# Four of the seven layer-1 products of the last four batches as seven inner products each

## The chip, the cores and the metric

The kernel runs on one core of a Trainium2 chip. The metric is the device time of one execution in microseconds (us); the times are medians of a few runs. All arithmetic is in 32-bit floats.

## The reference

An attention block with pooled queries is followed by a block in which each batch routes its 128 best tokens through a two-layer network.

```python
# attention: B, H, S, D = 8, 8, 1152, 64
q_pool = q.reshape(B, H, S // 2, 2, D).mean(axis=3)
attn = softmax(q_pool @ k^T / sqrt(D))
x = (attn @ v) as (B, 576, 512)
# mixture of depths: w1 is 512 x 1024, w2 is 1024 x 512, capacity 128
scores = np.einsum('bsd,d->bs', x, w_gate)
out = x.copy()
for b in range(B):
    top_idx = np.argpartition(-scores[b], capacity)[:capacity]
    xe = x[b, top_idx]
    h = np.maximum(xe @ w1, 0.0)
    ye = h @ w2
    g = 1.0 / (1.0 + np.exp(-scores[b, top_idx]))
    out[b, top_idx] = x[b, top_idx] + g[:, None] * ye
```

## The kernel before

The attention runs over 32 pairs of heads in two halves each (`run`); it takes some 572 us, and TensorE is busy all through. While it runs, the gate scores of each batch are summed, its tokens ranked, gathered (L1179) and turned into `xeT`, features on the partitions. The network of all eight batches is computed at the end, in `ending`, and this is the part that the change touches.

`ending` takes the batches in two groups of four, and in each group two pairs of batches form the two block rows of a matrix. A product of 2 x 2 blocks is made with seven block products instead of eight (Winograd's form of Strassen's method), with four sums of the inputs (S1 to S4), four sums of the weights (T1 to T4, made during the attention and kept in `tw` and, for layer 2, in `last_sums`), and seven additions of the results.

- Layer 1 of a group (`first_layer`): block rows are two pairs of batches, block columns of the input the two halves of the 512 features, block columns of the weights two halves of the 1024 hidden units. One block product (`first_product`, matmuls at L1271) has an input of 2 chunks x 128 features by 256 tokens and weights of 256 x 512. It is 8 matmuls of 128 x 128 weights and 256 columns, and a 32-bit matmul shows as two passes in the trace: 16 passes. Each product fills one PSUM tile of two banks. VectorE adds the results (`add`, L1298), ScalarE copies the first (L1311) and applies Relu to each finished quarter c11, c12, c22, c21 (L1309).
- Layer 2 (`second_of`, matmuls at L1285): for a pair of batches, seven products of 8 passes, 128 tokens by 256 outputs. ScalarE copies some (L1362, L1364), VectorE adds, multiplies by the gate and adds to the tokens (`scaled`, L1293). The last pair is written out at the end of `ending`.
- `input_sums` makes S1 to S4 of layer 1 on GpSimd (POOL, L1257); `four_sums` makes those of layer 2 on VectorE (L1351).
- `scattered` writes a pair's tokens to the output by two indirect DMAs of POOL (`written`, L1240).

PSUM holds four product tiles (`banks`, a pool of four buffers of two banks), taken in turn: a fifth product waits until the first one's tile is read. The order on every engine is the order in which the program issues (`manual_schedule`); the order is written out by hand, and `pieces` interleaves it: it steps through the generator of a layer, and at the steps numbered in `behind` it also issues a piece of the ranking of the last batch (`waiting`), whose last step is the transpose that completes the tokens of batch 7 (L1215). `counted` (L1511) and `outside` (L1526, a matmul of one column) test the softmax sums of all batches for a range; a rerun in another form follows if they leave it.

Most SBUF is used, so the rooms of the ending are tiles of the attention's pools taken again: `rooms[0]` and `rooms[1]` (two tiles of exponents) hold the quarters of the hidden layer, intermediate sums and the input sums of layer 2; `acc` holds the input sums of layer 1 and the intermediate results of layer 2.

Of the kernel before, what the change touches and what calls it, by code (L numbers as in the profile page):

```python
# [540 lines left out]
class _Plain:  # L541
# [707 lines left out]
    def input_sums(self, a, s):  # L1249

        a11, a12, a21, a22 = a
        s1, s2, s3, s4 = s
        add, subtract = ALU.add, ALU.subtract
        for to, x, y, op in (
            (s1, a21, a22, add), (s2, s1, a11, subtract), (s3, a11, a21, subtract), (s4, a12, s2, subtract)
        ):
            self.nc.gpsimd.tensor_tensor(out=to, in0=x, in1=y, op=op)  # L1257

# [38 lines left out]
    def add(self, to, x, y):  # L1297
        self.nc.vector.tensor_tensor(out=to, in0=x, in1=y, op=ALU.add)  # L1298
# [54 lines left out]
    def second_of(self, tokens, a, s, y):  # L1353

        copy, add = self.nc.scalar.copy, self.add
        half, w = self.Dm // 2, tokens[0]["w"]
        y1, y2, y7, y3, y4 = (y[0:w, i * half : (i + 1) * half] for i in range(5))
        to = [token["xe"][0:w, i * half : (i + 1) * half] for token in tokens for i in range(2)]
        one, two = tokens
        products = self.second_layer(a, s, (1, 2, 7, 3, 4, 5, 6))  # L1360
        for part in (y1, y2, y7):
            copy(part, next(products))  # L1362
            yield
        copy(y3, next(products))  # L1364
        add(y2, y2, y1)
        self.scaled(to[0], y2, one, to[0])
        yield
        add(y4, y1, next(products))
        add(y3, y3, y4)
        add(y4, y4, y7)  # L1370
        yield
        ps = next(products)
        add(y4, y4, ps)
        add(y7, y3, ps)
        yield
        add(y3, y3, next(products))
        for of, at, token in ((y3, to[1], one), (y4, to[2], two), (y7, to[3], two)):
            self.scaled(at, of, token, at)
        yield

    def ending(self, halves, old):
# [7 lines left out]
        def pieces(unit, n=None, of=1):  # L1389
            nonlocal done  # L1390
            for i, _ in enumerate(unit):
                for _ in range(of):
                    if done in behind:
                        next(waiting)
                    done += 1
                if i + 1 == n:
                    break
# [10 lines left out]
        def first(i):  # L1408
            x, y = (self.tokens[4 * i + 2 * j]["turned"] for j in range(2))
            a = [t[:, :, k * self.ND // 2 : (k + 1) * self.ND // 2, 0:w] for t in (x, y) for k in range(2)]  # L1410
            c = [self.hidden_of(rooms[i][:, k * n : (k + 1) * n], w) for k in range(4)]
            m = [self.hidden_of(room[:, 4 * n : 5 * n], w) for room in rooms]
            return a, c, self.first_layer(a, inputs, c, m)

        def second(i, j, c):
            a = [c[2 * j + k][:, :, t, :] for t in range(2) for k in range(2)]
# [15 lines left out]
        a, c, layer = first(0)  # L1432
# [9 lines left out]
        self.scored(halves[-1])  # L1442
        _, new, _ = self.routing.pop()
# [13 lines left out]
        pieces(self.second_of(*y, acc[1]))  # L1457
        a, c, layer = first(1)
        self.input_sums(a, inputs)
        self.scattered(y[0])  # L1460

        pieces(layer, 2)
        low = self.counted()
        pieces(layer, 2)
        outside = self.outside(low)
        pieces(layer, 1)
        x, y = second(1, 0, c), second(1, 1, c)
        self.four_sums(*x[1:])
        pieces(layer)
        layer = self.second_of(*x, acc[1])  # L1470
        pieces(layer, 3)
        self.four_sums(*y[1:])
# [221 lines left out]
```

## Time and profile before

| | us |
|---|---|
| median of the runs | 673.01 |
| lowest and highest run | 672.97, 673.38 |
| the profiled execution: time | 673.65 |
| the profiled execution: span | 671.9 |
| first layer-1 product of the second group starts, in the span | 617.40 |
| last product of TensorE ends, in the span | 666.2 |
| last scatter issued by POOL, in the span | 667.06 |

The span runs from the first to the last instruction of one execution; its time, 1.7 us longer, holds what lies around the span. PE is TensorE's matmuls and PEld its weight loads, which overlap them; DVE is VectorE, ACT ScalarE, POOL GpSimd, SP the engine that issues most DMAs. Times in the trace are us from the span's start. "[2.56 <-DVE acc L1298]" after an instruction says that its engine stood idle for 2.56 us before it and what ended the wait.

### The profile page before, as it was taken

To read this page: it belongs to the slowest core of one execution; us is meant where nothing else is said; L and a number is where in the kernel's file an instruction comes from. 1 tells how busy PE (TensorE), PEld (TensorE's weight loads), DVE (VectorE), ACT (ScalarE), POOL (GpSimd) and SP (SyncE) were. 2 spreads that over 40 slices of the span, in tenths; PEclk is the share of its full clock that TensorE was granted. 3 is DMA by queue.
4 is the path that set the end of the run, shared out by engine and by line. 5 is a ranking of instruction groups with operands and counts; after the bars stand their busy time and mean duration, and the time that the engine had idled before them with its cause. 6 is when DMAs were issued, how large, how long until landed. Compare 5 with 4: busy or idle time off the path is not lost.

```text
span 671.9 us, 22869 instructions
## 1 busy us (share of the span) xinstructions
PE 665.1 (99%) x9715; PEld 438.4 (65%) x9715; DVE 565.2 (84%) x811; ACT 441.2 (66%) x959; POOL 499.8 (74%) x465
## 2 busy tenths in 40 slices
PE   9999999999999999999999999999999999999996
PEld 6656666666666666666666666656666666888885
DVE  3878999998999987998899888988898899596463
ACT  5677778777777777778777777777777874221120
POOL 5788888889888988899888978898889877302302
PEclk9999999999999999999999999999999999999999
DMA  8989989868886788859866879588958845303001
GB/s 164 169 178 194 216 173 189 150 113 179 159 154 117 122 163 153 166 105 177 170 117 130 170 137 149 127 160 146 156 112 163 153 139 151 73 16 105 33 2 66
DMA packets 391048, 92.68 MB, mean 138 GB/s; under 512 B 371608, under 2 KB 376088, under 8 KB 390936
## 3 DMA queue, kind: packets, MB, share of 16 engines
q1 hardware_dynamic: 389496, 86.73, 67.1%
q0 software_dynamic: 1280, 4.20, 1.7%
q8 instruction: 78, 1.28, 0.8%
q14 instruction: 34, 0.28, 0.2%
q10 hardware_dynamic: 160, 0.20, 0.1%
HBM read 75.30 MB, written 15.79 MB: 136 GB/s over the span
## 4 chain that ended last, share of the span: by engine, by line
PE 92%; issue 5%; DMA 2%; POOL 1%; DVE 0%; POOLq 0%
PE ps L878 42%; PE ps L896 42%; PE ps L1285 4%; PE ps L1271 4%; DMA out_dram<-xe,index 1%; PE ps L623 1%; DMA out_dram<-v_sb,index 0%; POOL acc L1257 0%; POOL out_dram L1240 0%; PE ps L844 0%; DVE xe L1293 0%; POOL kT L1257 0%; DVE v_sb L1215 0%; PE ps L830 0%; DVE acc L1298 0%
## 5 line engine op out<-in xcount | busy, mean ns | idle before, releaser
L885 ACT ACTIVATE p<-ps 128x576 f32<-128x576 f32 x576 | 320.5, 699 | 2.2 <-PE ps L878 1.9
L917 POOL TENSOR_TENSOR acc<-p 128x576 f32<-128x576 f32 x192 | 283.0, 1501 | 38.3 <-ACT p L885 36.9
L878 PE MATMUL ps<-qT,kT 64*64 64x288 f32 x4608 | 292.0, 403 | 0.0
L896 PE MATMUL ps<-p,v_sb 64*64 64x288 f32 x4608 | 290.9, 403 | 0.0
L878 PEld LDWEIGHTS ps<-qT,kT 64*64 64x64 f32 x4608 | 174.1, 133 | 105.5 <-ACT p L885 13.4
L896 PEld LDWEIGHTS ps<-p,v_sb 64*64 64x64 f32 x4608 | 173.0, 133 | 106.6 <-ACT p L885 14.7
L922 DVE TRANSPOSE_TENSOR_REDUCE fold<-p 128x54 f32<-128x1728 f32 x64 | 126.3, 1974 | 44.3 <-ACT p L885 44.2
L904 ACT COPY two<-ps 128x576 f32<-128x576 f32 x64 | 40.8, 638 | 133.5 <-PE ps L896 131.6
L922 DVE TRANSPOSE_TENSOR_REDUCE fold<-acc 128x54 f32<-128x1728 f32 x64 | 124.5, 1945 | 3.7 <-POOL acc L917 3.5
L906 POOL TENSOR_TENSOR av<-two 128x288 f32<-128x288 f32 x64 | 51.3, 801 | 39.9 <-ACT two L904 39.0
L766 DVE STREAM_TRANSPOSE kT<-kb 128x1152 f32<-128x1152 f32 x31 | 73.9, 2385 | 0.0
L985 POOL TENSOR_TENSOR prod<-avb,w_gate 128x288 f32<-128x288 f32 x64 | 51.5, 805 | 0.0
L1116 DVE TENSOR_SCALAR_CACHE_REDUCE pick<-line 128x127 f32<-128x127 f32 (+4 forms) x80 | 45.2, 564 | 3.4 <-DMA line<-gate_lines 1.2
L763 POOL TENSOR_TENSOR qp<-qb 128x576 f32<-128x576 f32 (+1 forms) x32 | 43.9, 1373 | 5.5 <-DMA qb<-in_q_dram 3.9
L962 ACT ACTIVATE sums<-total,tiny 32x18 f32<-32x18 f32 x124 | 38.2, 308 | 1.9
L1240 POOL DMA_INDIRECT out_dram<-xe,index x7 | 6.9, 992 | 38.7 <-DVE xe L1293 28.2
L1021 POOL TENSOR_TENSOR x<-avb,rec 128x576 f32<-128x576 f32 x30 | 34.8, 1161 | 0.0
L1309 ACT ACTIVATE p<-p 128x1024 f32<-128x1024 f32 x8 | 8.5, 1058 | 39.0 <-DVE p L1298 33.5
L975 DVE STREAM_TRANSPOSE avb<-av 128x288 f32<-128x288 f32 x64 | 28.3, 442 | 3.8 <-POOL av L906 3.8
L1043 DVE TENSOR_REDUCE red<-prod 128x9 f32<-128x288 f32 x64 | 27.8, 435 | 2.7 <-POOL prod L985 2.7
L947 ACT COPY groups<-sum 32x36 f32<-32x36 f32 x124 | 27.2, 219 | 1.6
L1298 DVE TENSOR_TENSOR p<-p,ps 128x1024 f32<-128x1024 f32 x14 | 16.9, 1216 | 11.9 <-PE ps L1271 11.8
(103 smaller groups left out, 420.7 us busy)
## 6 DMA issues: line engine op xcount, KB each, us to landing
kb<-in_k_dram SPq DMA_DIRECT2D x124, 144.0 KB, 4.7
qb<-in_q_dram SPq DMA_DIRECT2D x124, 144.0 KB, 4.5
v_sb<-in_v_dram SPq DMA_DIRECT2D x31, 576.0 KB, 5.1
out_dram<-x SPq DMA_DIRECT2D x128, 72.0 KB, 5.0
lines<-row_rank SPq DMA_DIRECT2D x8, 640.0 KB, 4.2
w<-in_moe_w_dram SPq DMA_DIRECT2D x8, 512.0 KB, 4.7
line<-gate_lines SPq DMA_DIRECT2D x8, 351.5 KB
tw<-tw SPq DMA_DIRECT2D x4, 512.0 KB, 5.7
```

The costliest lines, as they stand in the source:

```text
L763: nc.gpsimd.tensor_tensor(out=qp[:, of, :], in0=pair["q"][:, of, 0, :], in1=pair["q"][:, of, 1, :], op=ALU.add)
L766: nc.vector.transpose(kT.rearrange("p (c i g) -> p c g i", c=self.NC, i=BLK), pair["k"].rearrange("p (g c) d -> p c g d", c=self.NC),)
L878: nc.tensor.matmul(sc[keys, j, 0:n], lhsT=pair["kT"][rows, c * P + keys.start : c * P + keys.stop], rhs=pair["qT"][rows, qs], start=True, ...
L885: nc.scalar.activation(p[:, c // G, c % G, :, :], sc[:, :, 0:n], AF.Exp, scale=self.scale)
L896: nc.tensor.matmul(av[j * self.D : (j + 1) * self.D, e, 0:n], lhsT=half["pair"]["v"][keys, j, c, :], rhs=half["p"][keys, c // G, c % G, j, :],
L904: nc.scalar.copy(two[:, :, :], av[:, :, 0:n])
L906: nc.gpsimd.tensor_tensor(out=half["av"][:, :], in0=two[:, 0, :], in1=two[:, 1, :], op=ALU.add)
L917: nc.gpsimd.tensor_tensor(out=acc[:, u, :], in0=units[:, 0, u, :], in1=units[:, 1, u, :], op=ALU.add)
L922: nc.vector.tensor_reduce(fold[:, a, :], of.rearrange("p u (m d) -> p (u m) d", d=BLK), AX.X, ALU.add, apply_transpose=True,)
L962: self.nc.scalar.activation(tot[rows, :], pair["total"][:, j * self.QB : (j + 1) * self.QB], AF.Identity, bias=self.tiny[0:BLK, 0:1],)
L985: self.nc.gpsimd.tensor_tensor(out=pair["prod"][:, ns, :], in0=pair["avb"][:, ns, :], in1=self.w_gate[:, hp : hp + 1, :].broadcast_to([P, ...
L1116: nc.vector.tensor_scalar(out=cmp[0:rows, 0 : part.stop - part.start], in0=near[0:rows, part], scalar1=sc[0:rows, t : t + 1], scalar2=None ...
```

## The change

The first group stays as it was in layer 1. In layer 1 of the second group `split` takes the place of `first_layer`. Four of its seven products (called one: a11 b11; two: a12 b21; six: S4 b22; seven: a22 T4) are themselves made as 2 x 2 block products with seven inner products each. An inner product (`inner_product`) has 128 features by 128 tokens and 256 hidden units: two matmuls of 128 columns, four passes. `inner_layer` issues the seven, in four banks of two PSUM tiles x and y, and adds them up on VectorE. The three others (S2 T2, S1 T1, S3 T3) stay whole. The inner weight sums (`inner_weights`, 16 adds on POOL into free tiles of the attention) are issued one at a time by `pieces`, from the first group's layer 1 on; the inner input sums (`inner_inputs`, four adds on POOL each) are issued as the layer goes. Larger sums of two products are added on POOL (`rest`), with Relu on ScalarE behind it. The order of products and sums in `second_of` is changed, the scatters of the first group's second pair and `counted` and `outside` are issued later, and the input sums of layer 2 for the next pair are split. Blank lines are left out.

```diff
--- before.py
+++ after.py
@@ -1246,15 +1246,77 @@
             oob_is_err=False,
         )
-    def input_sums(self, a, s):
+    def input_sums(self, a, s, which=slice(0, 4)):
         a11, a12, a21, a22 = a
         s1, s2, s3, s4 = s
         add, subtract = ALU.add, ALU.subtract
-        for to, x, y, op in (
-            (s1, a21, a22, add), (s2, s1, a11, subtract), (s3, a11, a21, subtract), (s4, a12, s2, subtract)
-        ):
+        steps = (s1, a21, a22, add), (s2, s1, a11, subtract), (s3, a11, a21, subtract), (s4, a12, s2, subtract)
+        for to, x, y, op in steps[which]:
             self.nc.gpsimd.tensor_tensor(out=to, in0=x, in1=y, op=op)
+    def quarter_rooms(self):
+        load, work = self.load, self.work
+        yield load.tile([P, self.QB, BLK], F32, name="qp", bufs=1)
+        for _ in range(2):
+            yield load.tile([P, self.Sp], F32, name="qT")
+        yield work.tile([P, self.QB, BLK], F32, name="prod", bufs=1)
+        for name in ("avb", "avb", "x", "x"):
+            yield work.tile([P, self.QB, BLK], F32, name=name)
+    def inner_weights(self, operands):
+        rooms = self.quarter_rooms()
+        n = self.F // 4
+        for operand in operands:
+            t = operand["t"] = []
+            b11, b12, b21, b22 = (operand["b"][:, k, j * n : (j + 1) * n] for k in range(2) for j in range(2))
+            for i in range(4):
+                if i % 2 == 0:
+                    room = next(rooms)
+                    room = self.row(room) if len(room.shape) > 2 else room
+                to = room[:, i % 2 * n : (i % 2 + 1) * n]
+                x, y = ((b12, b11), (b22, t[0] if t else None), (b22, b12), (b21, t[1] if i == 3 else None))[i]
+                self.nc.gpsimd.tensor_tensor(out=to, in0=x, in1=y, op=ALU.subtract)
+                t.append(to)
+                yield
+    def inner_inputs(self, operand):
+        room, w = operand["room"], operand["a"].shape[3]
+        a = [operand["a"][:, i, j, :] for i in range(2) for j in range(2)]
+        operand["s"] = [room[:, i * P : i * P + w] for i in range(4)]
+        self.input_sums(a, operand["s"])
+    def inner_product(self, tile, k, i, of, by):
+        to = tile[:, k, 2 * i * P : 2 * (i + 1) * P].rearrange("p (f n) -> p f n", n=P)[:, :, 0 : of.shape[1]]
+        for f in range(2):
+            self.nc.tensor.matmul(to[:, f, :], lhsT=by[:, f * P : (f + 1) * P], rhs=of, start=True, stop=True)
+        return to
+    def inner_layer(self, m, to, temps):
+        n = self.F // 4
+        product, add = self.inner_product, self.add
+        a11, a12, _, a22 = (m["a"][:, k, j, :] for k in range(2) for j in range(2))
+        b11, _, b21, b22 = (m["b"][:, k, j * n : (j + 1) * n] for k in range(2) for j in range(2))
+        (s1, s2, s3, s4), (t1, t2, t3, t4) = m["s"], m["t"]
+        c11, c12, c21, c22 = (to[:, 2 * i : 2 * i + 2, :] for i in range(4))
+        x, y = self.banks(), self.banks()
+        u, v = temps
+        self.nc.scalar.copy(u, product(x, 0, 0, a11, b11))
+        ps = product(y, 0, 0, s2, t2)
+        add(c11, u, product(x, 0, 1, a12, b21))
+        add(u, u, ps)
+        add(v, u, product(y, 1, 0, s1, t1))
+        ps = product(x, 1, 0, s3, t3)
+        add(c22, v, ps)
+        add(u, u, ps)
+        add(c12, v, product(y, 0, 1, s4, b22))
+        add(c21, u, product(x, 1, 1, a22, t4))
     def lines_of(self, room):
         return room.rearrange("p (c n) -> p c n", n=P)
@@ -1354,27 +1416,28 @@
         copy, add = self.nc.scalar.copy, self.add
         half, w = self.Dm // 2, tokens[0]["w"]
-        y1, y2, y7, y3, y4 = (y[0:w, i * half : (i + 1) * half] for i in range(5))
+        y1, y2, y5, y3, y4 = (y[0:w, i * half : (i + 1) * half] for i in range(5))
         to = [token["xe"][0:w, i * half : (i + 1) * half] for token in tokens for i in range(2)]
         one, two = tokens
-        products = self.second_layer(a, s, (1, 2, 7, 3, 4, 5, 6))
-        for part in (y1, y2, y7):
-            copy(part, next(products))
-            yield
-        copy(y3, next(products))
-        add(y2, y2, y1)
+        products = self.second_layer(a, s, (1, 5, 2, 7, 3, 4, 6))
+        copy(y1, next(products))
+        yield
+        copy(y5, next(products))
+        yield
+        add(y2, y1, next(products))
         self.scaled(to[0], y2, one, to[0])
         yield
+        add(y2, y5, next(products))
+        yield
+        copy(y3, next(products))
+        yield
         add(y4, y1, next(products))
+        add(y2, y2, y4)
         add(y3, y3, y4)
-        add(y4, y4, y7)
-        yield
-        ps = next(products)
-        add(y4, y4, ps)
-        add(y7, y3, ps)
+        add(y5, y5, y3)
         yield
         add(y3, y3, next(products))
-        for of, at, token in ((y3, to[1], one), (y4, to[2], two), (y7, to[3], two)):
+        for of, at, token in ((y3, to[1], one), (y2, to[2], two), (y5, to[3], two)):
             self.scaled(at, of, token, at)
         yield
@@ -1392,6 +1455,7 @@
                 for _ in range(of):
                     if done in behind:
                         next(waiting)
+                    next(weights, None)
                     done += 1
                 if i + 1 == n:
                     break
@@ -1405,15 +1469,76 @@
         def sums_room():
             return self.row(self.work.tile([P, G, 2 * self.HALF], F32, name="acc"))
-        def first(i):
-            x, y = (self.tokens[4 * i + 2 * j]["turned"] for j in range(2))
-            a = [t[:, :, k * self.ND // 2 : (k + 1) * self.ND // 2, 0:w] for t in (x, y) for k in range(2)]
-            c = [self.hidden_of(rooms[i][:, k * n : (k + 1) * n], w) for k in range(4)]
+        def halves_of(turned):
+            k = self.ND // 2
+            return turned[:, :, 0:k, 0:w], turned[:, :, k:, 0:w]
+        def first():
+            a = [half_of for token in self.tokens[0 : self.B // 2 : 2] for half_of in halves_of(token["turned"])]
+            c = [self.hidden_of(rooms[0][:, k * n : (k + 1) * n], w) for k in range(4)]
             m = [self.hidden_of(room[:, 4 * n : 5 * n], w) for room in rooms]
             return a, c, self.first_layer(a, inputs, c, m)
+        def lines(room):
+            return self.lines_of(room)[:, :, 0:w]
+        def across(room):
+            return room.rearrange("p (t f) n -> p f t n", t=2)
+        def rest(to, x, y, done=None):
+            nc.gpsimd.tensor_tensor(out=to, in0=x, in1=y, op=ALU.add)
+            if done is not None:
+                nc.scalar.activation(done, done, AF.Relu)
+        def hidden(to, x, y):
+            self.add(across(to), across(x), y)
+            nc.scalar.activation(to, to, AF.Relu)
+        def split(a):
+            u, v = (lines(room[:, 4 * n : 5 * n]) for room in rooms)
+            c11, c12, c21, c22 = c = [lines(rooms[1][:, k * n : (k + 1) * n]) for k in range(4)]
+            temps = [
+                [lines(rooms[0][:, k : k + half]) for k in (2 * n + 2 * i * half, 2 * n + (2 * i + 1) * half)]
+                for i in range(2)
+            ]
+            one, two, six, seven = operands
+            s1, s2, s3, s4 = inputs
+            t1, t2, t3, _ = (self.summed(1, i) for i in range(4))
+            x, product, add = second(1, 0, c), self.first_product, self.add
+            def layer():
+                self.inner_layer(one, u, temps[0])
+                yield
+                self.inner_layer(two, c11, temps[1])
+                yield
+                add(across(v), across(u), product(s2, t2))
+                rest(c11, c11, u, c11)
+                yield
+                add(across(c12), across(v), product(s1, t1))
+                self.input_sums(a, inputs, slice(3, 4))
+                self.inner_inputs(six)
+                self.input_sums(a, inputs, slice(2, 3))
+                self.inner_inputs(seven)
+                yield
+                self.inner_layer(six, u, temps[0])
+                yield
+                ps = product(s3, t3)
+                hidden(c22, c12, ps)
+                add(across(v), across(v), ps)
+                rest(c12, c12, u, c12)
+                yield
+                self.inner_layer(seven, c21, temps[1])
+                self.four_sums(*x[1:], slice(2, 3))
+                rest(c21, c21, v, c21)
+                yield
+            return c, x, layer()
         def second(i, j, c):
-            a = [c[2 * j + k][:, :, t, :] for t in range(2) for k in range(2)]
+            if i == 0:
+                a = [c[2 * j + k][:, :, t, :] for t in range(2) for k in range(2)]
+            else:
+                a = [c[2 * j + k][:, 4 * t : 4 * t + 4, :] for t in range(2) for k in range(2)]
             s = self.lines_in(rooms[1 - i][:, 2 * j * n : 2 * (j + 1) * n], self.NFC // 2, w, 4)
             return self.tokens[4 * i + 2 * j : 4 * i + 2 * j + 2], a, s
@@ -1429,7 +1554,7 @@
         self.drained(halves[-1])
         self.multiplied(halves[-2])
         rooms.append(exponents_room())
-        a, c, layer = first(0)
+        a, c, layer = first()
         self.input_sums(a, inputs)
         self.multiplied(halves[-1])
         self.scored(halves[-3])
@@ -1440,6 +1565,15 @@
         self.normalized(last)
         self.gated(halves[-1])
         self.scored(halves[-1])
+        operands = [
+            {"b": b, "room": room}
+            for b, room in zip(
+                (self.quarter(1, 0, 0), self.quarter(1, 1, 0), self.quarter(1, 1, 1), self.summed(1, 3)),
+                (*(rooms[0][:, k * n // 2 : (k + 1) * n // 2] for k in range(2)), rooms[0][:, n : n + n // 2],
+                 rooms[0][:, n + n // 2 : 2 * n]),
+            )
+        ]
+        weights = self.inner_weights(operands)
         _, new, _ = self.routing.pop()
         waiting = chain((None for _ in old), (None for _ in new), count())
         for of in (halves[-3]["pair"], last):
@@ -1454,21 +1588,26 @@
         self.four_sums(*y[1:])
         pieces(layer)
         self.scattered(x[0])
-        pieces(self.second_of(*y, acc[1]))
-        a, c, layer = first(1)
-        self.input_sums(a, inputs)
+        layer = self.second_of(*y, acc[1])
+        pieces(layer, 3)
+        operands[0]["a"], operands[1]["a"] = halves_of(self.tokens[self.B // 2]["turned"])
+        for operand in operands[:2]:
+            self.inner_inputs(operand)
+        pieces(layer)
+        a = [half_of for token in self.tokens[self.B // 2 :: 2] for half_of in halves_of(token["turned"])]
+        operands[2]["a"], operands[3]["a"] = inputs[3], a[3]
+        self.input_sums(a, inputs, slice(0, 2))
+        c, x, layer = split(a)
+        pieces(layer)
+        self.four_sums(*x[1:], slice(0, 2))
+        self.four_sums(*x[1:], slice(3, 4))
         self.scattered(y[0])
-
-        pieces(layer, 2)
-        low = self.counted()
-        pieces(layer, 2)
-        outside = self.outside(low)
-        pieces(layer, 1)
-        x, y = second(1, 0, c), second(1, 1, c)
-        self.four_sums(*x[1:])
-        pieces(layer)
+        y = second(1, 1, c)
         layer = self.second_of(*x, acc[1])
         pieces(layer, 3)
+        low = self.counted()
+        pieces(layer, 1)
+        outside = self.outside(low)
         self.four_sums(*y[1:])
         pieces(layer)
         self.scattered(x[0])
```

## The prediction

> **What bounds the kernel now.** I read the page's first part, then the busy time of the stretch that the change touches, then the order of instructions in it, engine by engine. The page's first part, and the two stretches from the start of the second group's layer 1 to TensorE's last product (columns: stretch, its length, busy time and count of each engine, granted clock, DMA):
>
> ```profile
> PE 665.1 (99%) x9715; PEld 438.4 (65%) x9715; DVE 565.2 (84%) x811; ACT 441.2 (66%) x959; POOL 499.8 (74%) x465
> ...
> 617.40:641.90 24.50, 24.50 (x116) 21.29 (x115) 13.74 (x22) 3.71 (x4) 7.72 (x7) 1.00 0.09 33
> 641.90:666.30 24.40, 24.32 (x113) 21.08 (x111) 13.22 (x27) 3.65 (x8) 2.93 (x3) 1.00 0.09 35
> ```
>
> TensorE has no idle time there: what is taken off its queue is won, and what makes it wait is lost in full, since only the last scatter (some 6 us) follows. The timeline of TensorE gives the products (start, length, engine, line, tiles, passes):
>
> ```profile
> 617.40 7.07 PE L1271 MATMUL ps<-xeT,w 128*128 128x256 f32 x32
> 624.30 7.07 PE L1271 MATMUL ps<-acc,tw 128*128 128x256 f32 x32
> 631.30 0.19 PE L1526 MATMUL ps<-low,ones 128*1 128x2 f32 x2
> 631.42 3.72 PE L1271 MATMUL ps<-kT,w 128*128 128x256 f32 x16
> ...
> 598.30 1.99 PE L1285 MATMUL ps<-kb,p 128*128 128x256 f32 x8
> 600.13 1.89 PE L1285 MATMUL ps<-qb,p 128*128 128x256 f32 x8
> ```
>
> Two products of layer 1 start 6.90 apart, so one takes 3.45 (16 passes of 0.216). A group of eight that starts after a wait lasts 1.99 instead of 1.89: a restart costs 0.1. The other engines in the same time, first VectorE and POOL around 618:
>
> ```profile
> 617.16 1.00 POOL L1240 DMA_INDIRECT out_dram<-xe,index  x1 [2.56 <-DVE acc L1298]
> ...
> 619.25 1.13 DVE L1215 STREAM_TRANSPOSE v_sb<-pick 128x512 f32<-128x512 f32 x1
> 620.53 1.27 POOL L1257 TENSOR_TENSOR acc<-v_sb 128x512 f32<-128x512 f32 x1 [2.38 <-DVE v_sb L1215]
> 621.88 1.27 POOL L1257 TENSOR_TENSOR acc<-acc,xeT 128x512 f32<-128x512 f32 x1
> ```
>
> POOL is held by the first group's scatters until 618.16, and batch 7's tokens are turned by 620.38; today S2 is ready at 623.15 and TensorE wants it at 624.3. Prices, from the groups and (last line) two passes of 128 columns at full clock early in the run:
>
> ```profile
> L1309 ACT ACTIVATE p<-p 128x1024 f32<-128x1024 f32 x8 | 8.5, 1058 | 39.0 <-DVE p L1298 33.5 <-DVE rank_parts L1107 5.5
> L1362 ACT COPY acc<-ps 128x256 f32<-128x256 f32 x9 | 3.1, 373 | 11.4 <-PE ps L1285 9.7 <-DVE xe L1293 1.7
> L1298 DVE TENSOR_TENSOR acc<-acc,ps 128x256 f32<-128x256 f32 x13 | 5.2, 418 | 9.2 <-PE ps L1285 9.1
> L1298 DVE TENSOR_TENSOR p<-p,ps 128x1024 f32<-128x1024 f32 x14 | 16.9, 1216 | 11.9 <-PE ps L1271 11.8
> L985 POOL TENSOR_TENSOR prod<-avb,w_gate 128x288 f32<-128x288 f32 x64 | 51.5, 805 | 0.0
> 9.40 0.38 PE L844 MATMUL ps<-ident,p 128*128 128x128 f32 x2
> ```
>
> The second of those two passes starts 0.38 - 0.27 = 0.11 after the first (one lasts 0.27): half of 0.216, so weight loads do not slow 128-column passes. POOL: 0.80 for 288 elements a partition and 1.27 for 512 make 2.1 ns an element: 0.47 for 128, 0.73 for 256, 2.35 for 1024.
>
> **What the Trainium skill says.** "PSUM — Partial Sum Buffer", section "PSUM bank collisions raise a hardware error": two engines must not touch one bank of the same partitions at once, even in different columns, and the kernel has to guard by bank. Before, no product tile is written again while it is read, so the trace has no example; in the change two inner products share a bank, and the second has to wait until the first is read. Same page, "Engine vs sequencer instructions": ScalarE's, VectorE's and GpSimd's queues are strict FIFO; the trace agrees, POOL stood 10.5 us before its L1132 for ScalarE. "GPSIMD Engine Reference", "3.1 Elementwise": a two-input add of 2048 takes 4497 ns, 2.2 ns an element, which supports the extrapolation to 1024. "TensorE: Matmul & The Clock Gate", "What's actually happening": after an idle window of about 3.4 us the clock is halved; this trace has it only at the start (twenty 128-column passes in 4.64 us, 0.22 each).
>
> **The change part by part.** All in microseconds on TensorE's queue.
>
> 1. *Products.* Four of seven products: 7 inner products of 4 passes, 28 x 0.108 = 3.02 instead of 3.45. **-1.7** in all. Layer 2 keeps its 14 products.
>
> 2. *Inner weight sums.* 16 POOL adds of 0.73 = 11.7, between 577 and 604, around waits of the ranking. POOL has almost nothing else there, and its gather comes at 609. They are wanted from 617 on: **0**. Were the cover gone, they would cost as far as they pass 617.
>
> 3. *New order of layer 2* (y5 before y2). Same products. The P4 tile is released by the add behind the token search, at 608.9, and the PSUM tiles go round in fours: y's third product wants that tile at 608.76. **+0.25** with the restart. Batch 7's transpose then ends near 620.75 (one VectorE add more in the chain before it).
>
> 4. *Inner input sums of products one and two.* Eight POOL adds (0.43 each back to back) queue behind the scatters, from 618.2. The second inner product needs its s2 at 618.1 but gets it at 619.2. **+1.2.** S1 and S2 follow and end at 624.3; they are wanted near 627.8.
>
> 5. *Inside one inner layer.* Banks in order: x0, y0, x0, y1, x1, y0, x1. From its first pass at 0: x00 is complete at 0.60, ScalarE's copy at 1.0, so the third product (bank x0 again) starts at 1.15 instead of 0.86: +0.29. VectorE's c11 add starts at 1.8, u + y00 ends at 2.55: the sixth product (bank y0 again) gives +0.24. Then v, c22, u + x10: dependent adds 0.48 apart, the last ends at 3.9, when the seventh (bank x1 again) may start: +0.86. 3.02 + 1.39 = 4.4, longer than the 3.45 of the plain product. In layer one the VectorE is busy with the transpose until 620.75 (+1.48, of other places), in seven the first wait belongs to step 6 (+1.1): 1.48 + 2 x 1.39 + 1.1 = **+5.4**.
>
> 6. *ScalarE's queue before layer seven.* Behind the S3·T3 product stand, one after the other: VectorE's c22 add 1.22, POOL's c12 + u 2.35 (it overwrites what that add reads), ScalarE's Relu of c12 1.06, and only then, in ScalarE's queue, the copy of seven's first inner product 0.37: 5.0, with the semaphores 5.3. Layer seven's third product needs that copy and would be ready 0.7 after S3·T3: **+4.6.** The same `rest` after S2·T2 (c11) is hidden: ScalarE has 3 us to spare there. POOL's S4, S3 and the eight sums for six and seven run from 630.9 to 637.1, ahead of their products at 634.7 and 642.6.
>
> 7. *Layer 2 of the first pair.* Its copies stand behind the Relu of c21 on ScalarE; the first scaled sum comes late, `counted` (1.55 of VectorE) ends at 659.1, and the one-column matmul of `outside`, now after the fourth product, waits at 658.2. Before, it cost 0.3. **+0.7.** S3 for P5 comes in time, because seven is so late; if seven were not, P5 would wait for it. The four sums for y (2.5) end by 662.4, before 664.4.
>
> 8. *Moved past queues.* The scatters of y (two descriptors of 1 us, 3.5 apart on POOL) come after layer 1 instead of during it; nothing waits for them before the last pair's. SP gets nothing new. The last pair is unchanged.
>
> Sum: -1.7 + 0.25 + 1.2 + 5.4 + 4.6 + 0.7 = **+10.4**. The profiled execution took 673.65 (span 671.9 and 1.7 around it) and would become 684.1; it lies 0.64 above the median of the runs, so against the median of 673.01 I predict **683.4 us**.
>
> Costs that the trace does not show: the bank wait lies between 0 (none) and 2.0 a layer (reads and writes wholly in turn), 1.39 taken; the halved clock between 0 and 1.7 (3.4 us at half speed, if the 4.6 us gap holds a whole idle window), 0 taken as the gap barely exceeds it; POOL's 1024-element add between 2.2 and 3.0 (POOL's L917 runs at 2.6 ns an element), 2.35 taken.
>
> **The rivals.** A: *no bank waits.* If TensorE may write a bank that is being read, step 5 vanishes, but seven's VectorE adds and the sums behind them still wait for ScalarE's copy, so P5 waits 4.2 instead: 677.5. For it speaks that only columns are shared; against it the skill's page. Chance 8%.
> B: *everything is hidden, faster.* The readers keep up with the inner products, in one place: ScalarE and VectorE empty a bank before TensorE returns to it. Then only -1.7 is left: 671.3. VectorE has just 7 x 0.42 = 2.9 of adds per inner layer against 3.02; it decides at a chain from third to seventh product below 1.3, and the rows above make it 2.1, and ScalarE would also have to be free at 643. Chance 6%.
> C: *the clock halves* during the gap in step 6: up to 685.1, and with slower POOL adds 686.5. Chance 18%.
> D: my forecast, 66%. What is left, 2%, is a net of nothing. That the change doesn't do what it says is excluded: the calls are unconditional.
>
> **How the numbers follow.** A measurement of this kernel tells 0.2% (1.3 us) from no change. Range: from 680.0 (bank waits half as long, or the ScalarE wait shorter) to 686.5 (C). Faster is B, 0.06; same 0.02; slower is A, C and D, 0.92.
>
> **What would show it.** Right: inner layers with 112 passes of 128 columns; waits of PEld for ScalarE and VectorE in L1271's successor, some 0.9 before the seventh inner product, and one near 4.6 in the last inner layer that ScalarE ends; POOL adds of 1024 elements near 2.35; TensorE's busy share in the layer down to 70%. Wrong: inner layers of 3.0 without gaps (A or B), a copy in layer seven that runs before the Relu of c12, or a TensorE clock below 1 there (C).

## The result, and the profile after

| | before | after |
|---|---|---|
| median of the runs, us | 673.11 (672.62 to 673.41) | 691.69 (690.25 to 692.32) |
| the profiled execution: time, span | 673.65, 671.9 | 690.25, 688.5 |
| layer 1 of the second group starts | 617.40 | 617.79 |
| layer 2 of the second group starts | 641.89 | 657.22 |
| TensorE's last product ends | 666.23 | 682.89 |

The ratio is 1.0274, 95% interval 1.0261 to 1.0287. The direction was forecast; the time lies 5 us beyond the upper end of the range, and the loss is 1.8 times the forecast one.

The page's first part after, and the two stretches that answer to those of before (stretch, length, busy time and count of PE, PEld, DVE, ACT and POOL, granted clock, DMA share, GB/s):

```profile
PE 668.8 (97%) x9763; PEld 441.6 (64%) x9763; DVE 579.3 (84%) x836; ACT 440.4 (64%) x959; POOL 529.6 (77%) x500
...
617.80:657.20 39.40, 28.73 (x161) 24.59 (x160) 19.06 (x37) 4.55 (x7) 17.54 (x23) 0.91 0.02 7
657.20:682.90 25.70, 24.75 (x116) 21.15 (x114) 18.33 (x36) 2.71 (x6) 7.88 (x6) 1.00 0.14 54
```

Layer 1 has grown from 24.5 to 39.4 us, with TensorE busy for 28.7 of them and its mean clock at 0.91; layer 2 has grown by 1.3. POOL has 30 us more work over the run. The view of TensorE's waits from 574 to 690 (who waited for whom: total, times, longest), which lists none for the kernel before from 574 to its end (a wait of 0.43 at 598.30 stands only in that kernel's timeline):

```profile
PE ps L1296 <- DVE p L1360: 5.1, 7, 1.5
PE ps L1296 <- ACT p L1310: 4.2, 1, 4.2
PE ps L1347 <- DVE p L1360: 1.3, 1, 1.3
PE ps L1296 <- POOL p L1256: 1.1, 1, 1.1
PE ps L1665 <- DVE pick L1650: 0.9, 1, 0.9
```

12.6 us in all. They are placed by TensorE's timeline (start, length, line, tiles, passes, wait before it); L1296 is an inner product's matmul, L1333 a whole product's, L1347 one of layer 2, L1665 that of `outside` (the numbers shift by a few lines from kernel to kernel):

```profile
617.79 0.61 PE L1296 MATMUL ps<-xeT,w 128*128 128x128 f32 x4
619.50 0.71 PE L1296 MATMUL ps<-p,qp 128*128 128x128 f32 x4 [1.11 <-POOL p L1256]
...
622.14 0.71 PE L1296 MATMUL ps<-p,qp 128*128 128x128 f32 x4 [1.48 <-DVE p L1360]
...
624.77 0.61 PE L1296 MATMUL ps<-xeT,w 128*128 128x128 f32 x4
625.22 0.61 PE L1296 MATMUL ps<-p,qT 128*128 128x128 f32 x4
625.84 0.71 PE L1296 MATMUL ps<-xeT,w 128*128 128x128 f32 x4
627.59 0.71 PE L1296 MATMUL ps<-p,qT 128*128 128x128 f32 x4 [1.04 <-DVE p L1360]
...
628.90 0.68 PE L1296 MATMUL ps<-p,w 128*128 128x128 f32 x4 [0.16 <-DVE p L1360]
...
630.22 7.07 PE L1333 MATMUL ps<-acc,tw 128*128 128x256 f32 x32
...
646.06 0.61 PE L1296 MATMUL ps<-v_sb,tw 128*128 128x128 f32 x4
646.50 0.61 PE L1296 MATMUL ps<-p,x 128*128 128x128 f32 x4
651.31 1.22 PE L1296 MATMUL ps<-v_sb,tw 128*128 128x128 f32 x4 [4.20 <-ACT p L1310]
653.58 2.08 PE L1296 MATMUL ps<-p,x 128*128 128x128 f32 x8 [1.04 <-DVE p L1360]
...
657.22 1.89 PE L1347 MATMUL ps<-w,p 128*128 128x256 f32 x8
...
665.23 0.19 PE L1665 MATMUL ps<-low,ones 128*1 128x2 f32 x2 [0.94 <-DVE pick L1650]
```

Layer one runs from 617.79 to 624.77, 6.98 us; two to 630.22, 5.45; six (637.13 to 642.60) 5.47; seven (646.06 to 657.22) 11.16. A whole product takes 3.45. An inner product without a wait takes 0.446 (four passes of 0.1115; 624.77 to 625.22 shows it), so seven of them take 3.12. The fourth inner product, s1 t1 (called y10, in bank 1 of tile y), has a wait of more than 1 us in every layer, and the prediction's list of waits inside a layer has none there. From 651.31 to 657 the passes last twice as long: 2.08 for eight, where eight in layer six take 1.16.

ScalarE, POOL and VectorE ahead of layer seven, each from its engine's timeline:

```profile
646.26 2.35 DVE L1360 TENSOR_TENSOR p<-p,ps 128x1024 f32<-128x1024 f32 x2 [3.03 <-PE ps L1333]
...
647.56 2.35 POOL L1489 TENSOR_TENSOR p<-p 128x1024 f32<-128x1024 f32 x1 [8.16 <-DVE p L1360]
...
649.95 1.06 ACT L1491 ACTIVATE p<-p 128x1024 f32<-128x1024 f32 x1 [1.38 <-POOL p L1489]
650.91 0.35 ACT L1310 COPY p<-ps 128x256 f32<-128x256 f32 x1
```

This is step 6 as it was written: add, POOL's sum, Relu, and only then the copy of an inner product that had been ready since 646.7; TensorE goes on at 651.31.

### The profile page after: what moved, and what is told of

It reads as the page before. It is cut to its first block, busy times and chain, and to the rows that moved or that the text cites. A ratio compares the mean times of both kernels' runs of the same rounds, so it can differ in the third digit from the quotient of the medians.

```text
span 688.5 us, 23050 instructions
## 1 busy us (share of the span) xinstructions
PE 668.8 (97%) x9763; PEld 441.6 (64%) x9763; DVE 579.3 (84%) x836; ACT 440.4 (64%) x959; POOL 529.6 (77%) x500
## 3 DMA queue, kind: packets, MB, share of 16 engines
q8 instruction: 78, 1.28, 0.8%
## 4 chain that ended last, share of the span: by engine, by line
PE 88%; DVE 3%; issue 3%; DMA 2%; POOL 1%; SPq 1%; ACT 0%; POOLq 0%; DVEq 0%
PE ps L878 41%; PE ps L896 41%; PE ps L1347 3%; PE ps L1333 2%; DVE p L1360 2%; DMA out_dram<-xe,index 1%; PE ps L1296 1%; SPq L1032 1%; PE ps L623 1%; DVE p L1413 1%; DVE pick L1116 1%; DMA line<-gate_lines 0%; POOL p L1489 0%; DMA out_dram<-v_sb,index 0%; POOL acc L1256 0%
## 5 line engine op out<-in xcount | busy, mean ns | idle before, releaser
L878 PEld LDWEIGHTS ps<-qT,kT 64*64 64x64 f32 x4608 | 174.3, 133 | 105.2 <-ACT p L885 13.8
L1360 DVE TENSOR_TENSOR p<-p,ps 128x256 f32<-128x256 f32 (+1 forms) x39 | 24.6, 644 | 22.5 <-PE ps L1296 11.1
L1489 POOL TENSOR_TENSOR p<-p 128x1024 f32<-128x1024 f32 x3 | 7.4, 2479 | 22.1 <-DVE p L1360 22.1
L932 DVE TENSOR_REDUCE sum<-fold 128x18 f32<-128x108 f32 x64 | 21.7, 339 | 2.2
```

The costliest lines, as they stand in the source:

```text
L878: nc.tensor.matmul(sc[keys, j, 0:n], lhsT=pair["kT"][rows, c * P + keys.start : c * P + keys.stop], rhs=pair["qT"][rows, qs], start=True, ...
```

## The experiments

The kernel before ran beside each set of experiments: 673.96 us with the first four, 673.37 with the next four, 673.06 and 673.08 with the rest. Ratios are to it. The changed kernel's 1.0274 was taken beside 673.11, so kernels of different sets are compared by their ratios; with the intervals as they are, a difference from the changed kernel of less than some 1.4 us is not told from noise. Unless it is said, a kernel is the changed one with one edit.

**Whole products again (`whole`).** Do the inner layers carry the loss, or the rest of the change?

```diff
-                self.inner_layer(one, u, temps[0])
+                nc.scalar.copy(across(u), product(one["a"], one["b"]))
```

and so for two, six and seven; the inner sums of weights and inputs are left out with them, as nothing reads them.

> The changed kernel's order, with products one, two, six and seven made whole again by one product and one ScalarE copy each; no inner sums of weights or inputs. If the inner layers carry the loss, TensorE's layer 1 is back at 24.2 us, only a wait of 1 to 2 us at the one-column matmul is left, and the time is 674 to 676. If the new order of the frame (sums, scatters, second layer) carries it, the time stays above 682.

Measured: 676.38, ratio 1.0035 (1.0022 to 1.0048), 0.4 above the range expected. So the inner layers with their sums carry 16 of the 18.6 us (2.4 are left over the kernel before). The new order of layer 2 costs nothing in the first group: from the first group's second layer-1 product to the second group's first takes 41.51 here and 41.74 before. What is left is the late count, in TensorE's timeline:

```profile
650.09 0.19 PE L1661 MATMUL ps<-low,ones 128*1 128x2 f32 x2 [2.10 <-DVE pick L1646]
650.21 3.60 PE L1347 MATMUL ps<-kb,p 128*128 128x256 f32 x8
```

After this one wait of 2.10 us eight passes take 3.60 us instead of 1.89: the clock is halved for one product.

**The fourth inner product in a tile of its own (`y10_apart`).** Theory: the program guards a PSUM tile as a whole, and y10 waits until y00, in the other bank of the same tile, is read. Rival: the banks are guarded one by one, and y10 waits for something else.

```diff
-        add(v, u, product(y, 1, 0, s1, t1))
+        add(v, u, product(self.banks(), 0, 0, s1, t1))
```

> The changed kernel, with the fourth inner product (y10) in a third PSUM tile of its own instead of the second bank of tile y. Theory T (the program guards whole product tiles, so y10 waits until y00 in the other bank of its tile is read): y10's wait of 1.0 to 1.5 us goes, x10 waits about 0.3 for the read of x01 instead, an inner layer falls from 5.45 to about 4.7 us, the time by some 3 us to 688.5. Theory B (guards by bank, as the prediction had it): y10 shares no bank in either kernel, so nothing changes, 691.7.

Measured: 687.84, ratio 1.0210 (1.0193 to 1.0227). Layer two on TensorE, from its third product on:

```profile
625.81 0.71 PE L1296 MATMUL ps<-xeT,w 128*128 128x128 f32 x4
626.36 0.61 PE L1296 MATMUL ps<-p,qT 128*128 128x128 f32 x4
627.19 0.68 PE L1296 MATMUL ps<-p,prod 128*128 128x128 f32 x4 [0.23 <-DVE p L1360]
...
628.94 0.71 PE L1296 MATMUL ps<-xeT,prod 128*128 128x128 f32 x4 [0.61 <-DVE p L1360]
```

y10 (626.36) no longer waits; layer two takes 4.75 instead of 5.45. So the program's guard takes in both banks of a tile.

**A tile for every inner product (`four_tiles`).** The same for all seven, in the rotation of four tiles, so that none shares one with a product still to be read.

> Every inner product gets a two-bank PSUM tile of its own, in a rotation of four, instead of two tiles shared by seven products; all else as in the changed kernel. If the loss inside an inner layer is the whole-tile guard (theory), the inner layers two and six fall from 5.45 us to 3.3-3.7 us, layer one to about 5 (its first wait and the scaled adds of VectorE stay), the 4.2 us hole of layer seven stays but is split over two products, and the time falls by 6 to 7 us, to 684-686. If VectorE's seven adds or the latency from an add to the next product are the bound (rival), the inner layers stay at 4.4 us or more and the time at 687 or more.

Measured: 682.10, ratio 1.0127 (1.0111 to 1.0144), 9.9 us under the changed kernel by the ratios, where 6 to 7 were expected. Six falls to 3.19 (633.97 to 637.16), two to 3.65, one to 4.99; the rival, VectorE's adds as the bound, would have kept them above 4.4. Seven still takes 8.04, but that is 3.1 less than in the changed kernel, where the whole hole was expected to stay; its waits stand where four tiles put them:

```profile
643.39 0.68 PE L1296 MATMUL ps<-p,x 128*128 128x128 f32 x4 [1.20 <-DVE p L1359]
646.04 1.20 PE L1296 MATMUL ps<-p,x 128*128 128x128 f32 x4 [1.97 <-ACT p L1309]
```

**The Relus behind the copy (`relus_late`).** Step 6 by itself: the Relus of c22 and c12 are issued after layer seven.

```diff
-                hidden(c22, c12, ps)
+                add(across(c22), across(c12), ps)
...
-                rest(c12, c12, u, c12)
+                rest(c12, c12, u)
                 yield
                 self.inner_layer(seven, c21, temps[1])
+                for to in (c22, c12):
+                    nc.scalar.activation(to, to, AF.Relu)
```

> The changed kernel, with the Relus of c22 and c12 issued on ScalarE after layer seven's copy instead of before it. Theory Q (the copy stands behind POOL's sum in ScalarE's queue): the wait of 4.4 before the third product of layer seven falls to 0.3; VectorE's two large adds then still hold the fourth product, so 3.7 us come off, and another 1.5 to 3 if TensorE's clock no longer drops in layer seven: 685 to 688. Rival (PSUM tiles or the input sums of seven hold that product, not the queue): the wait stays near 4, 691.

Measured: 688.13, ratio 1.0202 (1.0185 to 1.0219). Layer seven takes 6.02 (649.32 to 655.34) instead of 11.16, and the hole before its third product is gone:

```profile
650.39 0.71 PE L1296 MATMUL ps<-v_sb,tw 128*128 128x128 f32 x4
652.71 1.16 PE L1296 MATMUL ps<-p,x 128*128 128x128 f32 x8 [1.61 <-DVE p L1360]
```

The queue was the cause. Layer seven wins 5.1 us in the profiled execution, and the ratio falls by 0.0072, 4.8 us. The halved clock is not gone: in this execution it lies in layer one instead (624.3 to 628).

**The hole filled (`spare`).** Nine more inner products that nothing reads are issued in layer seven's hole. If the clock falls because of the hole, layer seven runs at full clock and is shorter by what the clock cost.

```diff
+        for _ in range(m.get("spare", 0)):
+            product(y, 1, 0, s1, t1)
         add(c11, u, product(x, 0, 1, a12, b21))
```

> The changed kernel, with nine spare inner products (36 passes of 128 columns, some 4.0 us) put into layer seven's wait, written into a place that y10 overwrites. Clock theory (the 4.4 us gap halves TensorE's clock for what follows): the clock stays at 1.0 in layer seven, its passes stay 0.112 apart instead of 0.214, and the time falls by 1.5 to 3 us to 689 to 690. Rival (the slower passes come from something else in that stretch): no change or, where the spare work is not hidden, up to 1 us slower.

Measured: 690.72, ratio 1.0245 (1.0228 to 1.0262). Layer seven did what was expected: from its third product to layer 2 it takes 4.38 (654.35 to 658.73) instead of 5.91, so the halved clock cost 1.5 there. By the ratios the kernel is 2.0 us below the changed one, the size that was expected, though the two intervals just overlap. The profiled execution does not show that gain: at 693.17 it is the slowest of the four (the others took 689.87 to 691.14), and its clock fell in layer one:

```profile
620.52 0.71 PE L1296 MATMUL ps<-p,qp 128*128 128x128 f32 x4 [1.11 <-POOL p L1256]
621.07 0.61 PE L1296 MATMUL ps<-xeT,w 128*128 128x128 f32 x4
623.15 1.22 PE L1296 MATMUL ps<-p,qp 128*128 128x128 f32 x4 [1.48 <-DVE p L1362]
...
649.53 4.63 PE L1296 MATMUL ps<-p,x 128*128 128x128 f32 x40
654.35 0.71 PE L1296 MATMUL ps<-v_sb,tw 128*128 128x128 f32 x4 [0.19 <-ACT p L1310]
...
658.73 1.89 PE L1349 MATMUL ps<-w,p 128*128 128x256 f32 x8
```

From 623.15 on the passes take twice as long, after two waits of 1.11 and 1.48. The changed kernel's own profiled execution had the same two waits and full clock after them. So where the clock falls differs between executions with equal waits; the runs of the changed kernel have mean clocks of 0.992 to 0.995.

**Weight sums apart from VectorE's (`early_weights`).** Twelve of the sixteen inner weight sums are issued at once before the first group's four sums, the last four in the second group's layer 1.

> Twelve of the sixteen inner weight sums are issued in one go before the first four-sum group of VectorE, the last four in layer 1 of the second group, so that none runs beside VectorE's SBUF adds. If GpSimd's adds slow VectorE's (theory), the two groups of four sums come back from 4.0 us to 2.6 us, layer 1 of the second group starts at about 616.5 us instead of 617.8, and the time falls by 1.0-1.5 us, to about 690.3. If the late start comes from something else (rival), it stays at 617.8 and the time within 0.3 us of the changed kernel, apart from what the clock does.

Measured: 691.42, ratio 1.0260 (1.0242 to 1.0277): the mechanism came, but the gain, 0.9 us by the ratios, is not told from noise. Both groups of four sums are back at 2.6, and from the first group's second product to the second group's layer 1 it takes 41.51 again instead of 43.00. But layer one then waited 0.70 and 2.07 where the changed kernel's waited 1.11 and 1.48, and the clock was halved in it and again in layer seven (mean 0.989 to 0.992 in all runs). So the price was asked again in a kernel without inner layers.

**The count early, no inner layers (`whole_low`), and with the weight sums (`low_weights`).** `whole` with `counted` issued after S2 T2 and `outside` after S1 T1; and the same with the sixteen weight sums put back, read by nothing.

```diff
                 rest(c11, c11, u, c11)
+                found.append(self.counted())
                 yield
                 add(across(c12), across(v), product(s1, t1))
+                found.append(self.outside(found[0]))
```

> The kernel with the new order of layer 2 and whole products in layer 1 (no inner layers), but the count of the limits is issued right after S2T2 and its matmul ahead of six. Theory: what that kernel lost to the one before (676.4 against 674.0) was the 2.1 us wait of this matmul and the 1.7 us that the half clock after it cost; both go, and the time is 672.2-673.5, a little below the kernel before. Rival: the new order of layer 2 itself costs, and another wait takes the place: 674.5-676.

Measured: 673.50, ratio 1.0003 (0.9995 to 1.0012). The 2.10 wait and the halved clock are gone: all that `whole` had lost. The forecast of a small gain was not met.

> Whole products in layer 1 and the count early (673.5 us), with the sixteen inner weight sums of GpSimd put back where the changed kernel has them, and read by nothing. If they cost through VectorE's four sums beside them (theory), the two groups of four sums take about 4.0 us each instead of 2.6, layer 1 of the second group starts 1.3-1.5 us later after the first group's second product than without them (41.5 us), and the time is 674.6-675.0. If GpSimd's sums are hidden, as forecast (rival), the time stays at 673.2-673.8.

Measured: 674.57, ratio 1.0022 (1.0014 to 1.0031); the intervals do not touch, and the difference of the ratios is 0.0019, 1.3 us (1.2 us over `whole_scans`, below, which is another kernel without these sums and was measured in the same set). VectorE's four sums without the weight sums (`whole_low`, first line) and with them (`low_weights`), and TensorE's wait that follows from the second:

```profile
589.48 2.62 DVE L1413 TENSOR_TENSOR p<-p 128x512 f32<-128x512 f32 x4
```

```profile
589.08 4.02 DVE L1413 TENSOR_TENSOR p<-p 128x512 f32<-128x512 f32 x4
...
598.91 1.99 PE L1347 MATMUL ps<-kT,p 128*128 128x256 f32 x8 [1.31 <-DVE p L1360]
```

The wait stands in the changed kernel too (1.29 at 598.69; 0.43 before). POOL's adds suffer as well: in the changed kernel those beside the four sums take 1.07 to 1.18 (589.51, 590.54), those beside nothing 0.73. VectorE's adds with one source in PSUM hardly change beside POOL's sums (1.21 at 578.38 and 1.27 at 580.72 in the changed kernel, 1.20 to 1.22 before). The Trainium skill has this, "SBUF — State Buffer", section "Who interferes with whom": a VectorE instruction with two SBUF inputs contends with a GpSimd instruction that reads SBUF. The runs agree, and the prediction had not looked there.

**All mended at once.** Three attempts to keep the inner layers. `improved` has four tiles, early weight sums, early count; the input sums of one and two ahead of the scatters; S1 T1 summed into c22's room, so that c12 needs nothing of S3 T3; three scaled adds of VectorE after layer one; Relus later.

> Inner layers with everything found so far mended: own PSUM tile for each inner product, weight sums apart from VectorE's four sums, input sums of one and two ahead of the scatters, the scaled adds of the last piece after inner layer one, c12 without a wait on S3T3 and so ahead of seven's copy, the Relu of c22 and of c21 later in ScalarE's queue, the count early. If the waits named are all there is (theory), layer 1 of the second group takes 22.8-24.3 us against 24.5 before, and the time is 670.5-673. If inner layers lose for a reason not named (rival), 675 or more.

Measured: 677.73, ratio 1.0057 (1.0038 to 1.0077), the rival's number; layer 1 takes 28.08. One takes 3.14, as seven products without a wait should; two loses 2.17 in one wait, behind the scaled adds, which take 3.28 beside POOL's sums instead of 1.28.

In `improved` TensorE still waited 1.16 at 599.28, as the line of gate scores came late and held up VectorE's first scan of the ranks, and with it the four sums. The control moves that scan behind the four sums (`whole_scans`, no inner layers):

> The same kernel without the weight sums, and with VectorE's first scan of the ranks put behind the four sums of the first batches instead of ahead of them, so that a late gate line cannot hold up the four sums. Where the gate line comes late, this takes up to 1.2 us of wait off the fourth product of layer 2; where it comes in time, nothing. Expected 672.9-673.6, not over 674; it is the control for the next kernel.

Measured: 673.41, ratio 1.0007 (1.0000 to 1.0013), as expected. On top of it `improved2`, with the four tiles, early weight sums and input sums of `improved`: scaled adds after layer two, S3 T3 ahead of six, one of its readers on ScalarE.

> Inner layers on top of the control: an own PSUM tile for each inner product, weight sums apart from VectorE's SBUF adds, the scaled adds of the last piece after inner layers one and two, S3T3 ahead of six with one of its two readers on ScalarE, the Relus of c12 and c22 behind seven's copy. If bank guards, queue order and VectorE's load are all that inner layers lose by (theory), layer 1 of the second group takes 22.9-24.0 us against 24.5 in the kernel before, and the time is 0.5-1.6 us under the control, 671.3-672.8. If VectorE or GpSimd cannot keep up with 28 small products whatever the order (rival), 673.5 or more.

Measured: 675.62, ratio 1.0037 (1.0024 to 1.0051): the rival's number, 2.2 us over the control. Layer 1 takes 26.78. Its two longest waits are 1.02 in layer six, for ScalarE's copy of S3 T3 (see the last section), and 0.74 at `outside`, whose count stands behind the scaled adds on VectorE. These are again slowed by POOL's sums; the same three scaled adds in `improved2` and, with POOL held back, in `improved3`:

```profile
625.57 3.85 DVE L1354 SCALAR_TENSOR_TENSOR xe<-acc,own_gate,xe 128x256 f32<-128x256 f32 x3
```

```profile
624.97 1.27 DVE L1354 SCALAR_TENSOR_TENSOR xe<-acc,own_gate,xe 128x256 f32<-128x256 f32 x3
```

`improved3` holds POOL back there (the scatter that waits for these adds is issued ahead of POOL's next sums), puts S3 T3 between S2 T2 and S1 T1, and makes seven into v's room.

> As the second mended version, but the scaled adds with GpSimd held back beside them (3.85 us there, 1.28 us alone), S3T3 between S2T2 and S1T1 so that its two readers run under a whole product, and seven made into the room of v. If queue order and the contention of VectorE and GpSimd are what is left (theory), layer 1 of the second group takes 23.3-24.3 us instead of 26.8, and the time is 672.0-673.2, level with the control (673.4) or up to 0.2% below it. If inner layers keep losing what they save (rival), 674 or more.

Measured: 673.73, ratio 1.0010 (1.0001 to 1.0018), between the two forecasts: 0.5 above the theory's range and 0.3 below the rival's. The two stretches:

```profile
616.90:641.50 24.60, 24.11 (x163) 22.05 (x162) 18.02 (x42) 3.56 (x6) 20.08 (x21) 1.00 0.07 24
641.50:666.00 24.50, 24.39 (x114) 21.18 (x112) 16.93 (x32) 4.71 (x8) 7.13 (x6) 1.00 0.12 45
```

15 us of waits and clock are gone, and the clock is 1.00. The inner layers take 3.14, 3.66, 3.51 and 3.68, 14.0 together; four whole products take 13.8. Against 12.5 without a wait, 1.5 us of short stalls are left, and they use up the saving. That no other order could remove them is not shown. No kernel here was measured faster than the one before.

## Why the prediction was right or wrong

The direction was right, and so were place and size of the waits of steps 4 and 6, and the place and, in part by luck, the size of step 7. The sum was not: +10.4 against +17.5 on TensorE's queue in the profiled execution. (Its end moved by 16.66, but the first group's second product started 0.87 earlier than before, at 574.79 instead of 575.66, ahead of the first instruction that the change adds.)

| step | forecast | measured | how |
|---|---|---|---|
| 1 products | -1.7 | -1.3 | 4 x (3.12 - 3.45) |
| 2 weight sums | 0 | +1.35 | 43.01 - 41.66, `low_weights` less `whole_low` |
| 3 order of layer 2 | +0.25 | -0.1 | 41.66 - 41.74, `whole_low` less before |
| 4 input sums of one and two | +1.2 | +1.2 | wait 1.11 and 0.1 of restart |
| 5 waits inside a layer | +5.4 | +9.5 | 29.06 of the four layers, less 4 x 3.12, less steps 4 and 6 and the clock |
| 6 ScalarE's queue | +4.6 | +4.4 | 651.31 less 646.95, where the second product (646.50) and its 0.446 end |
| 7 `outside` | +0.7 | +1.0 | layer 2 longer by 1.33, less the 0.3 that it had cost in layer 1 |
| halved clock | 0 | +1.5 | 5.91 - 4.38, `spare` |

- **Step 5 failed most, by 4.1.** The chain of adds was about right, the guard was not: the step let y10 start while y00 was unread, because they are in two banks. The program guards the tile, and the account of the kernel before already has a whole product wait for a tile and not for a bank. Layer two pays 2.33 over seven free products where 1.39 was forecast, and each of the four layers pays 0.9 to 1.2 more than its forecast. With y10 in a tile of its own layer two pays 1.63, near the forecast; with a tile for each product 0.5. The bound that the prediction gave, 2.0 a layer, was still below what came.
- **Step 2 failed.** "Hidden because POOL is free and the sums are early" asked only when they are needed, not what runs beside them. They hold up VectorE's SBUF adds, those delay the adds that free a PSUM tile, and TensorE waits 1.3 at 598.7. The step set this term at 0, and it measured +1.35.
- **The clock.** Rival C was named with its place and bound of 1.7, and came: 1.5 in layer seven. It was valued at 0 in the sum, on the ground that the gap barely holds an idle window of 3.4 us as the Trainium skill has it ("TensorE: Matmul & The Clock Gate", "What's actually happening"). The runs differ from it: waits shorter than that were followed by the halved clock, one of 2.10 in `whole`, two of 1.11 and 1.48 in `spare`. Where the threshold lies is not shown.
- **Step 1** took half of a 256-column pass, 0.108; the passes run at 0.1115.
- **Step 3**: the wait that it forecast did not come; -0.1 is no change.
- **Steps 4, 6 and 8** stood: 1.11 from POOL, 4.20 from ScalarE with POOL's sum at 2.35; after its last product the kernel takes 5.6 us, against 5.7 before.
- **Step 7** had the wait at `outside` (0.94), but not its cause in full. The step put the late first scaled sum down to ScalarE's copies behind the Relu of c21. These end at 662.28; VectorE's four sums, slowed by POOL's sum of c21 beside them (which itself takes 2.73 instead of 2.35), end 0.4 later, and the add that the first scaled sum needs follows at once:

```profile
657.76 4.96 DVE L1413 TENSOR_TENSOR p<-p 128x512 f32<-128x512 f32 x4
662.68 0.42 DVE L1360 TENSOR_TENSOR acc<-acc,ps 128x256 f32<-128x256 f32 x1
```

  Alone four such sums take 2.6. So the slowing of step 2 stands in this term too, and that its size came near the forecast is in part luck.

The rest of the gap between forecast and median is the executions': the profiled one, 690.25, was the fastest of the six, whose median is 691.69.

## What to carry to other kernels

In a program that guards PSUM by tiles, as this one does, a product split into smaller ones needs a tile for each piece that is still to be read (tiles of one bank, twice as many, were not tried), and the readers' queues ahead of it empty: an engine that is free on average is not free when a copy stands behind a Relu that waits for a third engine. Before giving work to GpSimd, look at what VectorE does at that moment; two-source SBUF adds on both slowed each other here. Seven small products for one large one could win at most 0.33 of 3.45 us, 1.3 in all four, and in the best attempt short stalls of 1.5 us were left.

## What was not expected of the hardware

- VectorE's SBUF adds beside POOL's adds: 4.0 to 5.0 instead of 2.6 us for four of 128x512, and up to 3.85 instead of 1.28 for three scaled adds of 128x256; POOL's 128x256 adds 1.01 to 1.29 instead of 0.73.
- The clock was halved after less idle time than the 3.4 us named above: in the 3.4 us before 623.15 in `spare` TensorE stood idle for some 2.3 (1.48 and the part of the 1.11 that falls in them). Equal waits did not halve it in the changed kernel's profiled execution.
- In `improved2` ScalarE's copy of S3 T3 ran only after VectorE's add from the same PSUM tile had ended (637.29 after 636.04 and 1.22), and six's fourth product waited 1.02 for it: two readers of one tile took turns. In `improved3` it is the other way round, the add behind the copy (631.90 after 630.86 and 1.01). Each time they ran in the order in which the program issues them; whether the program makes the second wait or something else does was not tried.
